# Gates by matmul, state tiles from chunk 2 on, a room of its own for the first x block, rows three deep, and a written plan of units

## The chip, the cores and the metric

One core of one Trainium2 chip runs the whole kernel in one launch. The metric is device time in microseconds (us): the median over runs of the same program. TensorE (PE) does matmuls into PSUM, VectorE (DVE) and ScalarE (ACT) work element by element, GpSimd (POOL) here mostly issues accumulating DMAs ("gathers"), and SyncE (SP) issues the other DMAs.

## What is computed

Sequence length S = 2048, width D = 1024, state width P = 1024, all in bf16. Two branches work on the same x and a gate g mixes them:

```python
g = sigmoid((x * gate_w).sum(-1, keepdims=True))
# branch A: a diagonal complex state space model
h = Lam_bar * h + x_t @ B_bar.T            # for t in range(2048)
a = 2 * (hseq @ Cmat.T).real + x * Dskip
# branch B: short convolution of k (4 taps), times v, then a long convolution by FFT
kv = short_conv(B_k) * B_v
y = irfft(rfft(kv, 2S) * rfft(ssm_k, 2S))[:S] + kv * ssm_D
b = x * y
out = g * a + (1 - g) * b
```

## The kernel before

The kernel has two phases.

The **chunk loop** does branch B's long convolution, eight chunks of 128 channels (loop at L906, the last chunk from L1003). In pass c it transforms chunk c+1 (`fwd_K`, `fwd_V`: matmuls psk and psv), multiplies the spectra of chunk c on VectorE (`products`: tiles G, wkh, BT, t), and transforms chunk c-1 back (`inverse`: matmuls psz), whose result goes through `cv` to the DRAM scratch `cv_scr`. The taps of chunk c+2 and its times-v stand between these. Between them stand tiles of branch A's input product: `Bu(i)` (L687) gives two half units ("tiles"), each 32 matmuls of 256 columns ("odd" and "even") and 4 or 8 small ones with `lamd`, evicted by ScalarE to U. Pass c >= 3 takes both tiles of `Bu(c - 3)`, the last chunk four tiles (`Bu(4)`, `Bu(5)`).

The **scan phase** (from L1029) does the rest of branch A. `order` (L672) lists 16 units (time block tb of 512 steps, state group g of 256 states); units 6 to 15 are left for this phase. `scan(tb, g)` (L720) is VectorE's recurrence over one unit: rotate (A, trn), four scan instructions (W), rotate back (hb), and the odd steps into U. Scan j is unit (j // 4, j % 4). `turn_C` (L1039) turns one of eight C tiles; ScalarE writes m, VectorE does the rest; two are run after each of scans 0 to 3. `Cy(tb, tl)` is an output row t_ = 4 tb + tl: 128 time steps, 32 matmuls psy of 512 columns, over the four scans of its block and all C tiles, evicted by `scale_a` with the gate as scale to ga.

Each row also needs branch B. `loads` (L784) brings the row of `cv_scr` to pbb and of x to xr; `scale_b` (L794) scales pbb by 1 - g and Dskip by g to gd (one buffer), and a gather adds gd to pbb; `finish` (L825) multiplies xr by pbb on VectorE, adds that to ga by another gather and stores ga. The gate of rows 0 to 7 is formed by `gate_products` (VectorE: gd = x row times gate_w) and `gate_sum` (ScalarE: a sum along the row, then two sigmoids); that of blocks 2 and 3 by `gate` (L654): 32 one-column matmuls with the transposed x block and `gwb`, then two sigmoids.

The order of each engine is fixed: `put` (L91) chains every instruction of an engine behind the one before it, in the order in which the program text emits them. So what the generators and the loop at L1128 emit first goes first, and an instruction that waits holds up everything behind it on its engine. `between` (L1088) puts up to two finishes and one gate product into a scan; `prepare` puts the gate sum and `scale_b` behind a scan; `on_pe` (L1123) lists TensorE's units, taken at 1.3 per scan.

Rooms: `xt_pool` (L78) has three buffers in turn for the angle table h, the two-chunk loads v2, the x blocks and U2. When the chunk loop's pools close (L1028), the pools of the scan phase are laid over them in the order m, lam2, uu2, hb, io, wk.

Of the kernel before, what the change touches and what calls it, by code (L numbers as in the profile page):

```python
# [20 lines left out]
def kernel(  # L21
# [38 lines left out]
    TB = 512  # L60
# [16 lines left out]
    bt_pool = pool("bt", 1)  # L77
    xt_pool = pool("xt", 3)  # L78
    uu = pool("uu", 2), pool("uv", 4)
# [133 lines left out]

    def load_xT(tb, home=None, halves=(0, 1)):
        if 0 in halves:
            xTs[tb] = (home or xt_pool).tile([128, ND, TB], BF16, name="xT", tag="xT")
        for h in halves:
            load_t(xTs[tb][:, :, h * HB:(h + 1) * HB], xf[tb * TB + h:(tb + 1) * TB:2, :])
# [98 lines left out]
    def inverse_angles():  # L317

        hi = inv["room"] = xt_pool.tile([128, 2, 512], F32, name="h", tag="xT")
        for fi in range(2):  # L320
            act(hi[:, fi], trow[0], func=ACT.Identity, scale=inv["col"][:, fi:fi + 1], bias=inv["at0"][:, fi:fi + 1])
        yield
        rq = u4([128, 1024], F32, "rq")
        ts(rq, flat(hi), MAGIC, -MAGIC, ALU.add, ALU.add)
        yield
        tt(flat(hi), flat(hi), rq, ALU.subtract)
# [305 lines left out]
    omg = consts.tile([128, NT], F32, name="omg")  # L632
    gsum = consts.tile([128, NT], F32, name="gsum")
    gds = {}
    hbs = {}
# [5 lines left out]
    def gates_of(c4, sums):  # L641
        act(gcols[:, c4], sums, func=ACT.Sigmoid)
        act(omg[:, c4], sums, func=ACT.Sigmoid, scale=-1.0)

    def gate_products(t_):
        xw = gds[t_] = s5p["io"].tile([128, D], BF16, name="gd", bufs=1)
        tt(xw, ios[t_][1], rows_, ALU.mult)

    def gate_sum(t_):
        xw = gds.pop(t_)  # L650
        act(xw, xw, func=ACT.Copy, accum_out=gsum[:, t_:t_ + 1])
        gates_of(slice(t_, t_ + 1), gsum[:, t_:t_ + 1])

# [33 lines left out]
    def Bu(i):  # L687
        tb, g = order[i]
        if i in (10, 11):
            if i == 10:  # L690
                s5p["u2"] = xt_pool.tile([128, 2, 2, 2, 2, HB], BF16, name="U2", tag="xT")
            U = s5p["u2"][:, i - 10]
        else:
            home = uu[0 if i in (0, 1, 12, 13) else 1] if i < 6 or i in (12, 13) else s5p["uu"]
            U = home.tile([128, 2, 2, 2, HB], BF16, name="U")
        Us[tb, g] = U
        return [Bu_tile(tb, g, U, j) for j in range(2)]
# [96 lines left out]
    def scale_b(t_):  # L794
# [5 lines left out]
        else:  # L800
            gd = bt_row(3, t_ - NT + 4)
        act(gd, s5p["drow"], func=ACT.Identity, scale=gcols[:, t_:t_ + 1])
        gather(pbb, gd)
# [15 lines left out]
    def scale_a(t_, ps):  # L819
# [3 lines left out]
        gas[t_] = ga  # L823

    def finish(t_, ps=None):  # L825

        rows = rows_of(of, t_)
        pbb, xr = ios.pop(t_)
        tt(xr, xr, pbb, ALU.mult)
        if t_ < NT - 4:  # L830
            ga = gas.pop(t_)
            gather(ga, xr)
            yield
        elif ps is None:
            yield
# [15 lines left out]
    def step(gen):  # L851
        next(gen, None)
# [50 lines left out]

    old = none

    for c in range(NC - 1):  # L906
# [41 lines left out]
        run(old)  # L948
        if c == 1:
            load_BT(1, 0)  # L950
        elif c == 3:
            load("v", 6)
            load_BT(1, 1)
        elif c in (2, 4, 6):
            load_xT(c // 2 - 1)
        if nn < NC:
            dg = dgs(nn)
        bu = Bu(c - 3) if c >= 3 else (none, none)
        step(bu[0])
        fwd_K(n, (0, 1))  # L960
        step(bu[0])
        fwd_K(n, (2, 3))
# [9 lines left out]
        if nn < NC:  # L972
            tv = times_v(nn)
            step(tv)
            if nn + 1 < NC:
                load("kn", nn + 1)
                load("kT", nn + 1)
        step(bu[1])
        fwd_V(n, (0, 1))
        step(bu[1])  # L980
        fwd_V(n, (2, 3))
        if c < 3:
            lam_diag(c - 1, lam_pool)
# [19 lines left out]
    with tc.tile_pool(name="fin", bufs=1, side="right") as fin:  # L1003
# [9 lines left out]
        run(back)  # L1013
        b0, b1 = Bu(4)
        step(b0)
        step(b1)
        step(b0)
        run(prod)
        b2, b3 = Bu(5)
        step(b2)  # L1020
# [6 lines left out]
        run(back)  # L1027
    h3.close()  # L1028
    m_pool = pool("m", 3)  # L1029
    lam_pool2 = pool("lam2", 1)  # L1030
    s5p["uu"] = pool("uu2", 4)
    s5p["hb"] = pool("hb", 7)
    s5p["io"] = pool("io", 2)
    wk = pool("wk", 6)

# [11 lines left out]

    move(rows_, bc(gate_w.rearrange("(o d) -> o d", o=1), [128, D]))
    loads(0)
    s5p["drow"] = s5p["io"].tile([128, D], BF16, name="drow", bufs=1)  # L1050
    move(s5p["drow"], bc(A_Dskip.rearrange("(o d) -> o d", o=1), [128, D]))
    load_CT(range(4, NP), "ctb")
    for g in (2, 3):
        lam_diag(g, lam_pool2, g == 3)
# [28 lines left out]
    NS = NTB * NG  # L1083
    done = []

    rows = dict(loaded=1, prepared=0)

    def between():  # L1088
        t_ = rows["next"] = rows["prepared"] if rows["prepared"] < rows["loaded"] else None
        if t_ is not None and t_ < 2 * NG:  # L1090
            gate_products(t_)
        for t_ in [t_ for t_ in done if t_ < rows["prepared"]][:2]:
            done.remove(t_)
            yield from finish(t_)
            if rows["loaded"] < NT - 4:
                loads(rows["loaded"])
                rows["loaded"] += 1

    def prepare():
        t_ = rows["next"]  # L1100
        if t_ is not None:
            if t_ < 2 * NG:
                gate_sum(t_)
            scale_b(t_)
            rows["prepared"] += 1

    scans = [scan(j // NG, j % NG, between() if j > 0 else none) for j in range(NS)]

# [6 lines left out]
    def Cy_row(k):  # L1115
        Cy(k // NG, k % NG)
        done.append(k)

# [3 lines left out]
    Bu_next(7)  # L1122
    on_pe = ([(Bu_next, i) for i in range(8, 12)] + [(Cy_row, k) for k in range(4)]  # L1123
             + [(Bu_next, 12), (Bu_next, 13), (Cy_row, 4), (Bu_next, 14), (Cy_row, 5), (Bu_next, 15)]
             + [(Cy_row, k) for k in range(6, 12)])
    at = 0
    step(scans[0])
    for j in range(NS):  # L1128
        k = j - NG
        if 6 <= k < 10:  # L1130
            loads(k + 6)
        advance(j)
        for t in turning[2 * j:2 * j + 2]:
            run(t)
        on_act += [lambda t=t: step(t) for t in turning[2 * j + 3:2 * j + 5] for _ in range(2)]
        if j > 0:
            prepare()
        if j in (1, 2):
            loads(j)
            rows["loaded"] = j + 1  # L1140
        while at < len(on_pe) and at < (j + 1) * 1.3:
            f, i = on_pe[at]
            f(i)
            at += 1
        if 7 <= k < 11:
            scale_b(k + 5)
        if j == 0:
            load_xT(3)
        if k in (4, 5):
            gate(k - 2)  # L1150

# [7 lines left out]
    for g in range(NG - 1):  # L1159
        for tl in range(4):  # L1160
            Cy_g(tb, tl, pss[tl][0], g, False)
    while rows["prepared"] < NT - 4:
        rows["next"] = rows["prepared"]
        prepare()
    for t_ in done:
        run(finish(t_))
    fins = []
# [36 lines left out]
```

## Time and profile before

| | us |
|---|---|
| median of 3 runs (lowest, highest) | 440.94 (440.88, 442.83) |
| the profiled execution | 441.8 |
| its span | 439.9 |
| TensorE busy | 404.0 (92%) |
| VectorE busy | 389.8 (89%) |
| ScalarE busy | 259.0 (59%) |
| GpSimd busy | 50.4 (11%) |
| mean granted TensorE clock | 0.966 |

The page divides the span into 40 equal slices of 11 us; a digit is the busy share in tenths, 9 for 90% or more:

```profile
PE   7999796959999999989989998659999999999996
PEld 5556262626767667655858887324486765444442
DVE  8699999999979898999959926999789999999874
ACT  5797687876698777562348769611555651664201
POOL 3011120302012010100000001001110100231300
PEclk9999898989999999998989999879999999999998
```

The slices from about 253 to 297 us (the 24th to the 27th) hold the lowest VectorE digit of the page, TensorE's 8, 6 and 5, and a clock digit of 7; in nearly all other slices one of the two engines stands at 9 (8 in two or three). TensorE's matmuls overlap in their records, so a group's busy time can be a little more than the time it took; where matmuls follow each other without a gap, the distance from start to start is the cost of one.

### The profile page before, as it was taken

Reading aid. Unit: us, or ns where it says so; the run is one execution under the profiler, and the core shown is the slowest. Engines: PE = TensorE matmul, PEld = TensorE weight load, DVE = VectorE, ACT = ScalarE, POOL = GpSimd, SP = SyncE. Lnnn points to the kernel's source line nnn. Section 1 sums busy time; section 2 is a strip of 40 time slices with the busy share of each in tenths; the row PEclk is TensorE's granted clock in tenths of the full one; section 3 lists DMA queues with packets and bytes.
Section 4 is the critical chain, followed back from the end, with each engine's and each line's share of the span. In section 5 each row is a group of like instructions: output and inputs, shape, how many; then the busy total and the mean of one; then the engine's idle time right before and its main releaser. Section 6 shows DMA issues by size and latency. Waiting matters only on the chain.

```text
span 439.9 us, 7369 instructions
## 1 busy us (share of the span) xinstructions
PE 404.0 (92%) x2894; PEld 255.6 (58%) x2921; DVE 389.8 (89%) x643; ACT 259.0 (59%) x360; POOL 50.4 (11%) x71
## 2 busy tenths in 40 slices
PE   7999796959999999989989998659999999999996
PEld 5556262626767667655858887324486765444442
DVE  8699999999979898999959926999789999999874
ACT  5797687876698777562348769611555651664201
POOL 3011120302012010100000001001110100231300
PEclk9999898989999999998989999879999999999998
DMA  8889799896969981669939951114661535795802
GB/s 145 145 181 207 189 202 125 167 192 138 215 129 136 168 183 24 132 87 178 182 129 169 172 130 25 25 24 114 152 127 48 115 94 145 167 218 134 175 26 96
DMA packets 126149, 59.49 MB, mean 135 GB/s; under 512 B 106009, under 2 KB 112929, under 8 KB 126114
## 3 DMA queue, kind: packets, MB, share of 16 engines
q1 hardware_dynamic: 117808, 42.48, 47.1%
q0 software_dynamic: 8224, 16.52, 22.4%
q8 instruction: 23, 0.38, 0.4%
q14 instruction: 12, 0.10, 0.1%
q10 hardware_dynamic: 82, 0.02, 0.0%
HBM read 13.13 MB, written 8.39 MB: 49 GB/s over the span
## 4 chain that ended last, share of the span: by engine, by line
PE 56%; DVE 25%; issue 10%; DMA 4%; ACT 3%; SPq 1%; DVEq 0%; POOLq 0%
PE psy L93 24%; PE psk L93 7%; PE even L93 7%; DVE BT L93 5%; PE psz L93 5%; PE odd L93 5%; DVE G L93 5%; DVE wkh L93 5%; PE taps L93 4%; DVE t L93 3%; PE psv L93 3%; DMA kn<-in_B_ssm_k_dram 1%; DVE CT L93 1%; DVE W L93 1%; ACT Vh L93 1%
## 5 line engine op out<-in xcount | busy, mean ns | idle before, releaser
L93 PEld LDWEIGHTS <-BT 128*128 128x128 bf16 x1024 | 99.9, 98 | 15.5 <-issue 2.3
L93 PE MATMUL psy<-CT,hb 128*128 128x512 bf16 x249 | 60.9, 397 | 8.5 <-DVE CT L93 4.5
L93 PE MATMUL even<-xT,BT 128*128 128x256 bf16 x512 | 61.1, 273 | 2.0 <-ACT U L93 2.0
L93 PE MATMUL odd<-xT,BT 128*128 128x256 bf16 x512 | 61.1, 273 | 0.0
L93 PE MATMUL psy<-CT,U 128*128 128x512 bf16 x251 | 56.3, 379 | 0.3
L93 PEld LDWEIGHTS <-hb 128*128 128x128 bf16 x256 | 25.9, 101 | 40.4 <-issue 14.1
L93 PEld LDWEIGHTS <-U 128*128 128x128 bf16 x256 | 25.0, 98 | 29.8
L93 PE MATMUL psz<-G,CI 128*128 128x512 bf16 x64 | 28.4, 444 | 15.0 <-DVE G L93 14.9
L93 ACT ACTIVATE Vh<-psv 128x1024 bf16<-128x1024 f32 x32 | 30.9, 1038 | 7.9 <-PE psv L93 7.9
L93 DVE TENSOR_TENSOR_SCAN W<-rv,init,A 128x256 bf16<-128x256 f32 x48 | 32.1, 729 | 0.0
L93 ACT ACTIVATE U<-even 128x512 bf16<-128x512 f32 x32 | 19.0, 593 | 21.4 <-PE even L93 21.3
L93 PE MATMUL taps<-dg,kT 128*128 128x128 bf16 x512 | 31.6, 224 | 0.0
L93 PEld LDWEIGHTS <-SF 128*128 128x128 bf16 x192 | 18.8, 98 | 20.8 <-issue 1.9
L93 PEld LDWEIGHTS <-kT 128*128 128x128 bf16 x512 | 30.2, 101 | 0.9
L93 ACT ACTIVATE U<-odd 128x512 bf16<-128x512 f32 x32 | 18.9, 594 | 18.7 <-PE odd L93 18.2
L93 PE MATMUL psk<-eok,SF 128*128 128x512 bf16 (+1 forms) x128 | 29.4, 353 | 0.4
L93 ACT ACTIVATE cv<-psz 128x1024 bf16<-128x1024 f32 x16 | 16.5, 1030 | 22.5 <-PE psz L93 22.5
L93 PE MATMUL psz<-G,SI 128*128 128x512 bf16 x64 | 28.7, 449 | 0.0
L93 ACT ACTIVATE ga<-psy,gcols 128x1024 bf16<-128x1024 f32 x8 | 8.9, 1112 | 33.2 <-PE psy L93 33.2
L93 POOL DMA_DIRECT2D pbb<-gd x12 | 10.7, 888 | 134.5 <-PE odd L93 83.1
L93 DVE TENSOR_TENSOR U<-U,q 128x512 bf16<-128x512 bf16 (+2 forms) x51 | 23.5, 488 | 0.6
L93 ACT ACTIVATE BT<-psy,gcols 128x1024 bf16<-128x1024 f32 x5 | 5.5, 1109 | 29.9 <-PE psy L93 29.9
(169 smaller groups left out, 770.9 us busy)
## 6 DMA issues: line engine op xcount, KB each, us to landing
G<-wkh POOLq DMA_DIRECT2D x6, 768.0 KB, 8.1
cv_scr<-cv SPq DMA_DIRECT2D x16, 256.0 KB, 2.7
v<-in_B_v_dram SPq DMA_DIRECT2D x3, 1024.0 KB, 14.7
pbb<-cv_scr SPq DMA_DIRECT2D x12, 256.0 KB, 3.9
xr<-in_A_x_dram SPq DMA_DIRECT2D x12, 256.0 KB, 3.7
pbb<-gd POOLq DMA_DIRECT2D x12, 256.0 KB, 4.1
ga<-xr POOLq DMA_DIRECT2D x8, 256.0 KB, 3.3
out_dram<-ga SPq DMA_DIRECT2D x8, 256.0 KB, 2.8
```

The source lines that it names most:

```text
L93: i = f(*a, **kw)
```

## The change

- `gate_products` and `gate_sum` are gone with their tiles; all four blocks get their gate by `gate`: blocks 0 to 2 in the last chunk, behind the first state tile there, block 3 in the scan phase at j = 8. `rows_` now holds Dskip in place of gate_w.
- State tiles are drawn one by one from a single list: one in pass 2, one in pass 3, two in pass 4, one in pass 5, three in pass 6, four in the last chunk (0, 2, 2, 2, 2, 4 before).
- `xt_pool` is split into one buffer (`xt_first`: h, x block 0, x block 3) and two in turn (v2, x blocks 1 and 2, U2). x block 0 is loaded in pass 1, v 6 and the first half of BT 1 in pass 2.
- The pools of the scan phase are laid out in the order wk, lam2, hb, m, uu2 (five buffers in place of four), io.
- `between` is now one `product` (xr times pbb) per scan from scan 3 on; `Cy_row(k)` emits the row, then its sum and store (`combine`), then the loads of row k + 3 and the scaling of row k + 2. Rows 0 to 2 are loaded ahead.
- `plan` says which B units and rows stand behind each scan. Unit 12 comes ahead of row 0.

```diff
--- before.py
+++ after.py
@@ -75,7 +75,7 @@
     rot_pool = pool("rot", 1)
     lam_pool = pool("lam", 1)
     bt_pool = pool("bt", 1)
-    xt_pool = pool("xt", 3)
+    xt_first, xt_pool = pool("xta", 1), pool("xtb", 2)
     uu = pool("uu", 2), pool("uv", 4)
     psum = pool("psum", 4, space=bass.MemoryType.PSUM)
 
@@ -211,9 +211,9 @@
     def load_BT(g, c):
         load_t(BT[g][:, c], (A_B_re, A_B_im)[c][g * 256:(g + 1) * 256, :])
 
-    def load_xT(tb, home=None, halves=(0, 1)):
+    def load_xT(tb, halves=(0, 1)):
         if 0 in halves:
-            xTs[tb] = (home or xt_pool).tile([128, ND, TB], BF16, name="xT", tag="xT")
+            xTs[tb] = (xt_pool if tb in (1, 2) else xt_first).tile([128, ND, TB], BF16, name="xT", tag="xT")
         for h in halves:
             load_t(xTs[tb][:, :, h * HB:(h + 1) * HB], xf[tb * TB + h:(tb + 1) * TB:2, :])
 
@@ -316,7 +316,7 @@
 
     def inverse_angles():
 
-        hi = inv["room"] = xt_pool.tile([128, 2, 512], F32, name="h", tag="xT")
+        hi = inv["room"] = xt_first.tile([128, 2, 512], F32, name="h", tag="xT")
         for fi in range(2):
             act(hi[:, fi], trow[0], func=ACT.Identity, scale=inv["col"][:, fi:fi + 1], bias=inv["at0"][:, fi:fi + 1])
         yield
@@ -630,8 +630,6 @@
 
     gcols = consts.tile([128, NT], F32, name="gcols")
     omg = consts.tile([128, NT], F32, name="omg")
-    gsum = consts.tile([128, NT], F32, name="gsum")
-    gds = {}
     hbs = {}
     WL, init = {}, {}
     for tb in range(NTB):
@@ -641,15 +639,6 @@
     def gates_of(c4, sums):
         act(gcols[:, c4], sums, func=ACT.Sigmoid)
         act(omg[:, c4], sums, func=ACT.Sigmoid, scale=-1.0)
-
-    def gate_products(t_):
-        xw = gds[t_] = s5p["io"].tile([128, D], BF16, name="gd", bufs=1)
-        tt(xw, ios[t_][1], rows_, ALU.mult)
-
-    def gate_sum(t_):
-        xw = gds.pop(t_)
-        act(xw, xw, func=ACT.Copy, accum_out=gsum[:, t_:t_ + 1])
-        gates_of(slice(t_, t_ + 1), gsum[:, t_:t_ + 1])
 
     def gate(tb):
         psg = ps2([128, 2, 512], "p")[:, 0, 0:4]
@@ -691,7 +680,7 @@
                 s5p["u2"] = xt_pool.tile([128, 2, 2, 2, 2, HB], BF16, name="U2", tag="xT")
             U = s5p["u2"][:, i - 10]
         else:
-            home = uu[0 if i in (0, 1, 12, 13) else 1] if i < 6 or i in (12, 13) else s5p["uu"]
+            home = uu[0 if i in (0, 1, 13, 14) else 1] if i < 6 or i in (13, 14) else s5p["uu"]
             U = home.tile([128, 2, 2, 2, HB], BF16, name="U")
         Us[tb, g] = U
         return [Bu_tile(tb, g, U, j) for j in range(2)]
@@ -799,7 +788,7 @@
             gd = s5p["io"].tile([128, D], BF16, name="gd", bufs=1)
         else:
             gd = bt_row(3, t_ - NT + 4)
-        act(gd, s5p["drow"], func=ACT.Identity, scale=gcols[:, t_:t_ + 1])
+        act(gd, rows_, func=ACT.Identity, scale=gcols[:, t_:t_ + 1])
         gather(pbb, gd)
 
     def Cy_g(tb, tl, ps, g, last):
@@ -822,16 +811,21 @@
             act(ga[:, o], i, func=ACT.Identity, scale=gcols[:, t_:t_ + 1])
         gas[t_] = ga
 
+    def product(t_):
+        pbb, xr = ios[t_]
+        tt(xr, xr, pbb, ALU.mult)
+
+    def combine(t_):
+        ga = gas.pop(t_)
+        gather(ga, ios.pop(t_)[1])
+        move(rows_of(of, t_), ga)
+
     def finish(t_, ps=None):
 
         rows = rows_of(of, t_)
-        pbb, xr = ios.pop(t_)
-        tt(xr, xr, pbb, ALU.mult)
-        if t_ < NT - 4:
-            ga = gas.pop(t_)
-            gather(ga, xr)
-            yield
-        elif ps is None:
+        product(t_)
+        xr = ios.pop(t_)[1]
+        if ps is None:
             yield
             ga = gas.pop(t_)
             tt(ga, ga, xr, ALU.add)
@@ -902,6 +896,7 @@
     fwd_V(0, (2, 3))
 
     old = none
+    tiles = (b for i in range(6) for b in Bu(i))
 
     for c in range(NC - 1):
         n, nn = c + 1, c + 2
@@ -947,18 +942,20 @@
         run(back)
         run(old)
         if c == 1:
+            load_xT(0)
+        elif c == 2:
+            load("v", 6)
             load_BT(1, 0)
         elif c == 3:
-            load("v", 6)
             load_BT(1, 1)
-        elif c in (2, 4, 6):
+        elif c in (4, 6):
             load_xT(c // 2 - 1)
         if nn < NC:
             dg = dgs(nn)
-        bu = Bu(c - 3) if c >= 3 else (none, none)
-        step(bu[0])
+        bu = next(tiles) if c >= 3 else none
+        step(bu)
         fwd_K(n, (0, 1))
-        step(bu[0])
+        step(bu)
         fwd_K(n, (2, 3))
         step(prod)
         fk = none
@@ -975,10 +972,13 @@
             if nn + 1 < NC:
                 load("kn", nn + 1)
                 load("kT", nn + 1)
-        step(bu[1])
+        bu = [next(tiles) for _ in range({2: 1, 4: 1, 6: 2}.get(c, 0))] + [none, none]
+        step(bu[0])
         fwd_V(n, (0, 1))
+        step(bu[0])
         step(bu[1])
         fwd_V(n, (2, 3))
+        step(bu[1])
         if c < 3:
             lam_diag(c - 1, lam_pool)
         old = tabs
@@ -1011,12 +1011,13 @@
         run(old)
         steps(prod, 3)
         run(back)
-        b0, b1 = Bu(4)
+        b0, b1, b2, b3 = tiles
         step(b0)
+        for tb in range(3):
+            gate(tb)
         step(b1)
         step(b0)
         run(prod)
-        b2, b3 = Bu(5)
         step(b2)
         step(b1)
         step(b3)
@@ -1026,12 +1027,12 @@
         step(b3)
         run(back)
     h3.close()
+    wk = pool("wk", 6)
+    lam_pool2 = pool("lam2", 1)
+    s5p["hb"] = pool("hb", 7)
     m_pool = pool("m", 3)
-    lam_pool2 = pool("lam2", 1)
-    s5p["uu"] = pool("uu2", 4)
-    s5p["hb"] = pool("hb", 7)
+    s5p["uu"] = pool("uu2", 5)
     s5p["io"] = pool("io", 2)
-    wk = pool("wk", 6)
 
     def w2(shape, dt, name):
         return wk.tile(shape, dt, name=name, tag="w2")
@@ -1045,11 +1046,10 @@
             ts(CT[pi][:, c], CT[pi][:, c], f[:, pi:pi + 1], None, ALU.mult)
         tt(CT[pi], CT[pi], m, ALU.add)
 
-    move(rows_, bc(gate_w.rearrange("(o d) -> o d", o=1), [128, D]))
     loads(0)
-    s5p["drow"] = s5p["io"].tile([128, D], BF16, name="drow", bufs=1)
-    move(s5p["drow"], bc(A_Dskip.rearrange("(o d) -> o d", o=1), [128, D]))
+    move(rows_, bc(A_Dskip.rearrange("(o d) -> o d", o=1), [128, D]))
     load_CT(range(4, NP), "ctb")
+    loads(1)
     for g in (2, 3):
         lam_diag(g, lam_pool2, g == 3)
     late = []
@@ -1081,30 +1081,19 @@
 
 
     NS = NTB * NG
-    done = []
-
-    rows = dict(loaded=1, prepared=0)
+    rows = dict(scaled=0, multiplied=0)
 
     def between():
-        t_ = rows["next"] = rows["prepared"] if rows["prepared"] < rows["loaded"] else None
-        if t_ is not None and t_ < 2 * NG:
-            gate_products(t_)
-        for t_ in [t_ for t_ in done if t_ < rows["prepared"]][:2]:
-            done.remove(t_)
-            yield from finish(t_)
-            if rows["loaded"] < NT - 4:
-                loads(rows["loaded"])
-                rows["loaded"] += 1
+        if rows["multiplied"] < rows["scaled"]:
+            product(rows["multiplied"])
+            rows["multiplied"] += 1
+        yield
 
     def prepare():
-        t_ = rows["next"]
-        if t_ is not None:
-            if t_ < 2 * NG:
-                gate_sum(t_)
-            scale_b(t_)
-            rows["prepared"] += 1
-
-    scans = [scan(j // NG, j % NG, between() if j > 0 else none) for j in range(NS)]
+        scale_b(rows["scaled"])
+        rows["scaled"] += 1
+
+    scans = [scan(j // NG, j % NG, between() if j > 2 else none) for j in range(NS)]
 
     def advance(j):
         step(scans[j])
@@ -1114,40 +1103,36 @@
 
     def Cy_row(k):
         Cy(k // NG, k % NG)
-        done.append(k)
+        combine(k)
+        if k + 3 < NT - 4:
+            loads(k + 3)
+        if k + 2 < NT - 4:
+            prepare()
 
     turning = [turn_C(pi) for pi in range(NP)]
     on_act += [lambda t=t: step(t) for t in turning[0:3] for _ in range(2)]
     Bu_next(6)
     Bu_next(7)
-    on_pe = ([(Bu_next, i) for i in range(8, 12)] + [(Cy_row, k) for k in range(4)]
-             + [(Bu_next, 12), (Bu_next, 13), (Cy_row, 4), (Bu_next, 14), (Cy_row, 5), (Bu_next, 15)]
-             + [(Cy_row, k) for k in range(6, 12)])
-    at = 0
+    plan = ["B8", "B9 B10", "B11", "B12 C0", "C1", "C2", "C3", "B13", "C4 B14", "C5", "B15 C6", "C7", "C8", "C9", "C10", "C11"]
     step(scans[0])
     for j in range(NS):
-        k = j - NG
-        if 6 <= k < 10:
-            loads(k + 6)
+        if 10 <= j < 14:
+            loads(j + 2)
         advance(j)
         for t in turning[2 * j:2 * j + 2]:
             run(t)
         on_act += [lambda t=t: step(t) for t in turning[2 * j + 3:2 * j + 5] for _ in range(2)]
-        if j > 0:
+        for unit in plan[j].split():
+            (Bu_next if unit[0] == "B" else Cy_row)(int(unit[1:]))
+        if 0 < j < 3:
             prepare()
-        if j in (1, 2):
-            loads(j)
-            rows["loaded"] = j + 1
-        while at < len(on_pe) and at < (j + 1) * 1.3:
-            f, i = on_pe[at]
-            f(i)
-            at += 1
-        if 7 <= k < 11:
-            scale_b(k + 5)
+        if 11 <= j < 15:
+            scale_b(j + 1)
         if j == 0:
             load_xT(3)
-        if k in (4, 5):
-            gate(k - 2)
+            loads(2)
+        if j == 8:
+            gate(3)
 
     tb = NTB - 1
     t0 = tb * 4
@@ -1159,11 +1144,6 @@
     for g in range(NG - 1):
         for tl in range(4):
             Cy_g(tb, tl, pss[tl][0], g, False)
-    while rows["prepared"] < NT - 4:
-        rows["next"] = rows["prepared"]
-        prepare()
-    for t_ in done:
-        run(finish(t_))
     fins = []
     for tl in range(4):
         fins.append(finish(t0 + tl, None if tl == 1 else pss[tl][1]))
```

## The prediction

> **What bounds the kernel now.** I read three views: busy time by stage (stage borders at the inverse transforms of the chunks, at the end of the last product, 221.6 us, and at the first unbroken run of output rows, 294.6 us), then TensorE's and VectorE's instructions in order of time, then the chain of waits. Columns of the first: window, its length, busy us of PE, PE weight load, DVE, ACT, POOL with instruction counts, granted clock, DMA share, GB/s.
>
> ```profile
> 71.70:96.20 24.50, 19.41 (x131) 10.57 (x133) 24.43 (x27) 18.97 (x28) 3.95 (x5) 0.93 0.92 167
> 96.20:123.40 27.20, 27.09 (x203) 17.69 (x206) 25.48 (x27) 17.06 (x25) 3.95 (x5) 0.94 0.98 177
> 123.40:148.90 25.50, 25.39 (x204) 17.29 (x205) 23.51 (x20) 21.02 (x32) 3.95 (x5) 1.00 1.00 136
> 174.70:198.80 24.10, 21.49 (x146) 13.60 (x147) 22.63 (x20) 14.51 (x18) 1.20 (x1) 1.00 0.59 100
> 198.80:221.60 22.80, 20.86 (x168) 15.93 (x168) 22.70 (x19) 6.64 (x11) 0.00 (x0) 0.93 1.05 191
> 221.60:294.60 73.00, 62.76 (x515) 48.87 (x517) 54.95 (x116) 47.34 (x74) 2.61 (x3) 0.93 0.50 96
> 294.60:365.90 71.30, 70.15 (x536) 46.51 (x540) 64.47 (x145) 32.60 (x54) 9.50 (x11) 0.98 0.44 101
> 365.90:435.70 69.80, 69.42 (x324) 31.71 (x328) 61.10 (x138) 25.59 (x25) 12.06 (x14) 1.00 0.60 143
> ```
>
> In the chunk loop VectorE fills chunk 2 (24.43 of 24.50 us) and chunk 7, TensorE fills chunks 3 and 4. From 294.6 us TensorE is full to the end. The one stage that nobody fills is 221.6 to 294.6: 10 us of TensorE idle and 18 of VectorE. TensorE's idle there:
>
> ```profile
> 221.72 0.39 PE L93 MATMUL psz<-G,CI 128*128 128x512 bf16 x1 [2.06 <-DVE G L93]
> ...
> 274.78 1.91 PE L93 MATMUL even<-xT,BT 128*128 128x256 bf16 x16 [1.71 <-ACT U L93]
> ...
> 280.68 0.59 PE L93 MATMUL psy<-CT,hb 128*128 128x512 bf16 x1 [3.45 <-ACT U L93]
> ...
> 292.58 1.87 PE L93 MATMUL psy<-CT,hb 128*128 128x512 bf16 x4 [4.34 <-DVE CT L93]
> ```
>
> Output rows (psy) come too early: row 0 needs scans 0 to 3 and all eight turned C tiles, and VectorE is late with them. Why it is late, in its own order:
>
> ```profile
> 227.56 0.69 DVE L93 TENSOR_TENSOR A<-TCS,U 128x1024 bf16<-128x1024 bf16 x1 [4.92 <-PE psz L93]
> ...
> 267.91 0.69 DVE L93 TENSOR_TENSOR gd<-xr,rows 128x1024 bf16<-128x1024 bf16 x1 [12.40 <-ACT U L93]
> ...
> 320.86 0.69 DVE L93 TENSOR_TENSOR gd<-xr,rows 128x1024 bf16<-128x1024 bf16 x1 [4.76 <-issue]
> ```
>
> Scan 0 waits 4.92 us for the last inverse, whose tables lie in the room of its work tile; scan 2 waits 12.40 us for the single gd buffer. The chain shows that buffer's release:
>
> ```profile
> 264.62 3.21 DMA pbb<-gd
> 267.91 0.69 DVE gd L93
> ```
>
> The releaser printed (ACT U) had ended; the gather pbb<-gd ended last.
>
> **The change, part by part.** Let T0 be the end of the last product, 221.6 in this trace; the span ends 218.3 us later.
>
> *Gates.* Out go, for 8 rows, a VectorE product (0.60 us start to start), a ScalarE sum (1.05 + 0.19) and two sigmoids (0.2 each). In come gates of blocks 0 and 1 on TensorE, 32 one-column matmuls each: the two in the trace (blocks 2, 3) take 0.78 us from first to last start (349.51 to 350.29). Three stand in chunk 7: 2.35 us. TensorE's work there grows from 20.9 to 23.2, beside 22.9 of VectorE; the inverse that ends the stage waits 2.06 us in before, so this is hidden to within 0.3, and costs 2.35 if that wait is gone. The table load (1.28) moves there too, on a ScalarE busy 6.6 of 22.8 us. Gate 2 leaves the full stretch: -0.8.
>
> *State tiles from chunk 2 on.* A tile is 32 matmuls at 109 ns and 4 (block 0) or 8 small ones: 3.93 to 4.03 us. Per chunk 0,2,2,2,2,4 (chunks 2 to 7) become 1,1,2,1,3,4. Each chunk ends when both TensorE's transforms and VectorE's product are done, so I go chunk by chunk. Chunk 2: TensorE 19.4 + 3.9 = 23.3 beside 24.4, free (the 1.02 us that it waits there for ks<-lo is covered by the tile). Chunk 3: product 98.2 to 120.5, so the next inverse starts at 120.6 rather than 123.4: -2.8. Chunk 4, TensorE-bound, keeps 25.5. Chunk 5: TensorE 25.7 - 4.0 = 21.7, VectorE 22.4 from a start 1.3 us after the previous transform: another -2. Chunk 6 gives back: TensorE 21.6 + 4.0 = 25.6 beside 22.6. Carried through: last product starts at 196.2 instead of 198.6 (-2.4). But TensorE idles about 2 us before chunks 4 and 6, and rows of this trace halve the clock for 3.41 us after idles of 2.06 us and more (after 1.71 not): 1.7 each on a TensorE-bound chunk, so +0.9 at the other end. Bounds -2.5 to +0.9; I take -1.0.
>
> The Trainium skill, "TensorE: Matmul & The Clock Gate", Part 1, says that the half rate follows at least one idle window of about 3.4 us. By that the 2 us idles would cost nothing and this term would be -2.4; the trace has a halving after 2.06 us, so the row decides.
>
> *Transfers.* x block 0 (two transposes; SyncE's queue was held 11.3 us by them) moves ahead of kn 4 and kT 4 into chunk 1, in place of one B transpose (6.9): +4.4 to 5.6 us on those behind it. kT 4 left the queue at 72.2, lands about 4.6 later, and is used at 84.1: 7 us of cover. v 6 (1 MB, 14.7 to landing) moves from chunk 3 to 2, ahead of kn 5 and kT 5, whose cover is 10 us. Cost 0; without the cover up to 6. DMA share is 0.92 to 1.00 there, hence a rival.
>
> *Room order.* Scan 0's work tiles move off the tables: its instruction loses its wait on TensorE. VectorE starts 4.9 us earlier.
>
> *Rows.* xr*pbb now comes from scan 3 on, one per scan, and the finished scale of row k+2 is issued behind row k. The new wait: xr*pbb stands in VectorE's order, and behind it the rest of its scan. For row 0 ScalarE gets to it after tile pair B10, at T0+44.6 (inverse 4.15, then B6, B7 at 7.86, B8, B9 at 8.06, one and a half tiles more, an eviction); 2.2 to scale, 3.6 from there to VectorE as for row 0 above: T0+50.4. VectorE, free of gd, reaches it at T0+41.0: 0.85 for the lamd tile, 13.7 for scan 0 (227.56 to 241.26 here), twice 12.95 (241.26 to 254.82 less the gd product), 0.6. So it still waits, 9.4 us.
>
> *Plan of units.* B12 goes ahead of row 0: TensorE has 4.15 + 15.7 + 32.2 + 8.1 = 60.2 us of work before rows. VectorE after that wait ends scan 3 and the last two turns (2.05 each) 12.8 later, T0+63.2. Row 0 wants C tile 7 after 24 matmuls at 216 ns, T0+65.4. So the idles of the stage go: 0.25 + 1.71 + 3.45 + 0.22 + 4.34 + 0.19 + 0.91 = -11.1. With them go the half-rate clocks that follow the two long ones (280.5 to 283.9 and 290.8 to 297.6): 10.24 us at half, -5.1.
>
> Next late: scans take 9.8 us (10.15 with a carry), rows 6.9, B pairs 8.06. Rows 4 and 5 start at 95.9 and 111.6; scan 7's state is there at 99.9, wanted at 101.6: fits. xr*pbb of rows 7 and 8 waits for rows 5 and 6 plus 7.3 (1.1 eviction, 2.2 scales, 4.0 gather): 2.6 and 5.8 us. So scan 11's state comes at T0+148, and row 8 wants it at T0+145.6: +2.4 idle. Bounds 0 (a landing of 3.2, other waits absorbed) to 6 (landing 5.1 three times in a row). The last scan ends at T0+190, its state wanted at T0+192: TensorE sets the end.
>
> Sum on this execution: 439.9 - 1.0 - 11.1 - 5.1 - 0.8 + 2.4 = 424.3 us of span. 1.9 us lie around the span (441.8), and the median of the three runs is 0.9 below that run: **425 us**.
>
> **Rivals.**
> *All cover holds*: no idle at row 8, conversion of chunk gains in full, no halving before the last inverse (1.7): 424.3 - 2.4 - 1.4 - 1.7 = 418.8, 420 as a run. For: 2 us margins in the sums. Against: three margins under 2.5 us have all to hold. 0.12.
> *The round trip sets VectorE*: row, eviction, scale, gather, product, scan. With landings of 8.6 us (eok<-lo in the chunk loop) in place of 3.6 to 4.1, row 0 waits 2.8 for C tile 7, row 4 about 3, row 8 about 7: 13 in place of 2.4, and the clock is halved after them (3.4): 439 as a run at the worst, 436 with one absorbed. For: new waits on VectorE's path. Against: DMA share is 0.44 to 0.60 in these stages. 0.12.
> *A late kT or x block in chunks 2 to 5*: +4 to 6, 430. x block 1 landed about 0.4 us before its use in chunk 5. 0.08.
> *Slower*: gathers on POOL starve while VectorE runs. Then each of 12 products stops VectorE for a whole issue and landing, 0.86 + 3.3 = 4.2 us: 50 us less 4 of slack, 471. It passes before's time from (440.9 - 425.3 + 4) / 12 = 1.6 us per product. For: products were off this path before. Against: POOL's issue takes 0.86 us with VectorE full and 0.90 with it idle:
>
> ```profile
> 264.62 0.90 POOL L93 DMA_DIRECT2D pbb<-gd  x1 [83.14 <-PE odd L93]
> ```
> ```profile
> 374.97 0.86 POOL L93 DMA_DIRECT2D ga<-xr  x1 [9.99 <-ACT ga L93]
> ```
>
> 0.07. (The Trainium skill, "SBUF — State Buffer", section "SBUF: two separate sides", states such a rule: a VectorE mode that takes both ports locks GpSimd out, and its DMAs wait for their descriptors. The two rows don't show it.)
>
> **How the numbers follow.** Forecast 0.61 (421 to 429), and as above. 0.5% (2.2 us) is about what a measurement tells from no change: faster 0.90, same 0.03 (the round trip just past its worst), slower 0.07. The range 418 to 437 takes in the first rival and the round trip and leaves out the slow one.
>
> **What would show it.** Right: the idles at 274 to 294 are gone; VectorE stands about 9 us before the first xr*pbb; one idle of 1 to 4 us in row 8; TensorE full from T0+5; chunk 3 ends near 120.6; T0 within 219 to 222.5. Wrong: an idle before row 0 (VectorE's sum was short), a wait on kT or xT in chunks 2 to 5, landings over 5 us in the rows, or clock halvings with no idle of 2 us before them.

## The result and the profile after

The kernel after takes 428.69 us (median of 4 runs, 424.40 to 431.18); the kernel before, beside it, 441.88. The ratio is 0.967, 95% interval 0.958 to 0.975; it is taken of the fast runs alone, which leaves out the slow run of 431.18. A second set of six runs later gave 430.88 (427.89 to 432.71) beside 440.94: 0.978, 0.973 to 0.982. So it is faster by 2 to 4%, and its runs spread by 7 us.

The profiled run is one of the fastest: 424.40 us, with a span of 422.6 us against the 424.3 of span that the forecast's sum gave. Its stages, cut at its own borders; first in the chunk loop (chunks 3, 4 and 6), then from the end of the last product, 221.1 us, on. Columns as in the prediction: window, its length, busy us of PE, PE weight load, DVE, ACT, POOL with counts, granted clock, DMA share, GB/s.

```profile
95.30:119.70 24.40, 21.62 (x167) 13.63 (x169) 24.33 (x27) 21.34 (x33) 3.95 (x5) 1.00 1.18 194
119.70:147.30 27.60, 25.61 (x204) 17.23 (x207) 23.48 (x21) 20.13 (x30) 3.95 (x5) 1.00 1.02 126
...
170.80:198.20 27.40, 25.46 (x183) 17.24 (x186) 23.55 (x21) 14.62 (x19) 1.20 (x1) 1.00 0.80 87
...
221.10:294.60 73.50, 73.33 (x629) 58.39 (x632) 64.20 (x139) 45.60 (x66) 3.47 (x4) 1.00 0.53 99
294.60:365.90 71.30, 71.03 (x483) 43.47 (x487) 62.93 (x139) 29.63 (x35) 11.13 (x13) 1.00 0.60 137
```

The stage that nobody filled is full now: 73.33 of 73.50 us of TensorE where before had 62.76 of 73.00, and the clock in it is 1.00 instead of 0.93. Chunk 3 has become short (24.4 us, 27.2 before), but chunks 4 and 6 have become long (27.6 and 27.4, 25.5 and 24.1 before); chunk 6 also has one tile more than before. TensorE in order of time, last column the idle before the instruction and its releaser:

```profile
280.65 2.54 PE L93 MATMUL psy<-CT,hb 128*128 128x512 bf16 x10
```
```profile
368.04 2.33 PE L93 MATMUL psy<-CT,hb 128*128 128x512 bf16 x9 [1.28 <-DVE hb L93]
```

Row 0 starts with no idle before it, and of all idles behind the last product one is left, 1.28 us in row 8. VectorE, the two places that matter:

```profile
140.72 1.23 DVE L93 TENSOR_TENSOR G<-G,wkh 128x2048 bf16<-128x2048 bf16 x1 [4.09 <-DMA G<-wkh]
```
```profile
271.03 0.69 DVE L93 TENSOR_TENSOR xr<-xr,pbb 128x1024 bf16<-128x1024 bf16 x1 [7.46 <-DMA pbb<-gd]
```

The first is new: in chunk 4 the product waits for its own gather. The second is the wait for the first row's gather, which the prediction put at 9.4 us.

A reading that all the rest uses: call T0 the end of the last product on VectorE. The span is T0 plus the stage behind it. Busy time by stage (same columns) of the kernel after:

```profile
0.00:221.10 221.10, 200.10 (x1617) 128.94 (x1633) 207.70 (x246) 155.69 (x214) 26.24 (x43) 0.98 0.95 156
221.10:422.60 201.50, 195.22 (x1340) 124.66 (x1352) 177.97 (x391) 93.40 (x118) 24.02 (x28) 1.00 0.57 123
```

Before: T0 221.66, VectorE busy 207.91 of it, and 218.24 us behind it. So nearly the whole gain (16.7 us of 17.3 in the profiled runs) comes from behind T0, and up to T0 VectorE works for 207.7 us and waits for the other 13.4. T0 moves with waits.

### The profile page after: what moved, and what is told of

The parts are those of the page before. It is cut to its first block, busy times and chain, and to the rows that moved or that the text cites. A ratio compares the mean times of both kernels' runs of the same rounds, so it can differ in the third digit from the quotient of the medians.

```text
span 422.6 us, 7462 instructions
## 1 busy us (share of the span) xinstructions
PE 395.3 (94%) x2957; PEld 253.6 (60%) x2985; DVE 385.7 (91%) x635; ACT 249.1 (59%) x332; POOL 50.3 (12%) x71
## 4 chain that ended last, share of the span: by engine, by line
DVE 35%; issue 34%; PE 16%; DMA 11%; POOL 2%; ACT 2%; DVEq 0%; POOLq 0%; SPq 0%
DMA G<-wkh 8%; DVE BT L93 7%; PE psy L93 6%; DVE wkh L93 6%; DVE G L93 6%; DVE t L93 4%; PE psk L93 3%; DVE W L93 2%; DMA pbb<-cv_scr 2%; PE psz L93 2%; DVE hb L93 1%; DVE A L93 1%; PE taps L93 1%; DVE q L93 1%; DVE trn L93 1%
## 5 line engine op out<-in xcount | busy, mean ns | idle before, releaser
L93 PEld LDWEIGHTS <-BT 128*128 128x128 bf16 x1024 | 100.0, 98 | 13.4
L93 PE MATMUL psy<-CT,hb 128*128 128x512 bf16 x249 | 56.8, 379 | 1.6 <-DVE hb L93 1.3
L93 PEld LDWEIGHTS <-hb 128*128 128x128 bf16 x256 | 24.8, 98 | 30.4 <-DVE hb L93 2.0
L93 PE MATMUL psz<-G,CI 128*128 128x512 bf16 x64 | 26.1, 408 | 16.2 <-DVE G L93 16.2
L93 PE MATMUL psz<-G,SI 128*128 128x512 bf16 x64 | 25.9, 404 | 0.0
L93 PEld LDWEIGHTS <-CI 128*128 128x128 bf16 x64 | 6.6, 103 | 26.6 <-DVE G L93 19.1
```

The costliest lines, as they stand in the source:

```text
L93: i = f(*a, **kw)
```

## The experiments

Each is cut by its T0 and the time behind it, read from its trace, as well as by its run time.

**State tiles as before**, within the kernel after:

```diff
-        bu = [next(tiles) for _ in range({2: 1, 4: 1, 6: 2}.get(c, 0))] + [none, none]
+        bu = [next(tiles) for _ in range({3: 1, 4: 1, 5: 1, 6: 1}.get(c, 0))] + [none, none]
```

> The changed kernel with the state tiles handed out as before (0, 2, 2, 2, 2, 4 in chunks 2 to 7). Theory: the new places give almost nothing, because in the changed kernel VectorE waits 4.09 and 3.75 us in chunks 4 and 6 for the gather G<-wkh that lands late; the end of the last product (221.0 us in the changed kernel's trace) moves by 0 to +2 us, the time by as much. Rival (the prediction's chunk sums without any loss): chunk 3 and 5 become TensorE-bound again, +2.5 to +5 us.

427.85 us (4 runs, 422.42 to 432.79), T0 225.73, behind it 201.5. No difference from 428.69 that the spread lets one see. In its trace T0 is 4.6 us later than in after, which is the rival's range and not the theory's, but the runs as a whole are no longer; and a transfer was late there (TensorE waits 4.12 us for kT). The places of the tiles are worth nothing that can be measured here.

**Rooms of the scan phase as before** (m, lam2, uu2, hb, io, wk):

```diff
-    wk = pool("wk", 6)
-    lam_pool2 = pool("lam2", 1)
...
+    s5p["io"] = pool("io", 2)
+    wk = pool("wk", 6)
```

> The changed kernel with the pools of the scan phase laid out in the old order, so scan 0 waits again some 4.9 us for the last inverse. Theory: the wait of 7.46 us before the first xr*pbb takes this up whole (it shrinks to about 2.6), time 0 +- 0.5 us. Rival: VectorE's early start is what gets row 0 its C tiles in time; row 0 then waits 2 to 3 us, with a halved clock after it +4 us.

431.62 us (426.54 to 434.4), T0 223.29, behind it 201.5: to 0.1 us the time of after. The order of the rooms changes nothing behind T0. Scan 0 waits for no inverse in this trace either, so the wait that the new order was to remove did not come back here, and what the expectation said of it was not put to the test. The pool uu2 keeps its fifth buffer in this run, so wk does not lie where it lay in the kernel before; whether that is why stays open.

**B12 behind row 3**, within the kernel after:

```diff
-    plan = ["B8", "B9 B10", "B11", "B12 C0", "C1", "C2", "C3", "B13", "C4 B14", "C5", "B15 C6", "C7", "C8", "C9", "C10", "C11"]
+    plan = ["B8", "B9 B10", "B11", "C0", "C1", "C2", "C3", "B12 B13", "C4 B14", "C5", "B15 C6", "C7", "C8", "C9", "C10", "C11"]
```

> The changed kernel with unit 12 behind row 3, where it stood before, and nothing else moved. Theory: row 0 reaches its last C tile 8 us earlier than VectorE has turned it, less a margin of 2.5: TensorE idles 5 to 6 us in row 0 and the clock is halved after it, +5 to +9 us. Rival: TensorE's work is the same and rows only trade places, 0 to +1 us.

435.77 us (435.01 to 438.02, 7 runs), behind T0 208.7, 7.2 more. TensorE in order of time:

```profile
287.79 1.86 PE L93 MATMUL psy<-CT,hb 128*128 128x512 bf16 x4 [3.61 <-DVE CT L93]
```

The idle on the C tiles in row 0 is back, 3.61 us, and a half-rate window of 3.41 us right behind it costs 1.7 more. Another 1.7 of the 7.2 is a half-rate window from 226.3 us on, behind an idle of 2.26 us before the last inverse, and has nothing to do with B12. In this row pipeline B12 ahead of row 0 is needed.

**Gates from TensorE alone**, in the kernel before: old tiles, rooms, rows and order of units.

```diff
         step(b0)
+        for tb in range(3):
+            gate(tb)
         step(b1)
...
-        if t_ is not None and t_ < 2 * NG:
-            gate_products(t_)
...
-            if t_ < 2 * NG:
-                gate_sum(t_)
...
-        if k in (4, 5):
-            gate(k - 2)
+        if k == 5:
+            gate(3)
```

> The kernel before with one part of the change: gates of blocks 0 to 2 by matmul in the last chunk, of block 3 in the scan phase, no gate product on VectorE and no sum on ScalarE (the broadcast load of gate_w stays, unused). Theory: the 12.40 us wait of VectorE was for the gd buffer of the gate product alone, so it goes, row 0 finds its C tiles within 0 to 3 us, and this part alone brings 10 to 15 us of the 17 between the two profiled spans: 427 to 432. Rival: the wait moves to xr*pbb, and the plan of units and the rows in a pipeline carry the gain; this part alone brings 4 to 8 us: 434 to 438.

425.06 us (423.49 to 428.94), ratio 0.965 (0.959 to 0.972): as fast as the whole change or faster, and below the range of either forecast. T0 225.35, behind it 201.8, and TensorE has no idle at all there, though B12 stands behind row 3 as before. VectorE's wait of 5.13 us for the last inverse, which is gone in after, is still there and leaves TensorE without an idle.

**A tile of its own for the gates' product**, in the kernel before, gates left where they were:

```diff
-        xw = gds[t_] = s5p["io"].tile([128, D], BF16, name="gd", bufs=1)
+        xw = gds[t_] = s5p["io"].tile([128, D], BF16, name="gp", bufs=1)
```

> The kernel before, with one edit: the gates' product x*gate_w gets a tile of its own, so that it no longer waits until the gather pbb<-gd has read the single gd buffer. The gates stay on VectorE and ScalarE. Theory A (the gates cost by that wait and the TensorE idles and half-rate clocks behind it, not by their work): the 12.40 us wait of VectorE before the second product shrinks to under 3 us, the stage from the end of the last product to the end of the kernel, 218.2 us in before and 201.8 with the gates on TensorE, comes to 202 to 207 us. Theory B (the work itself costs: eight sums and sigmoids on ScalarE ahead of the state evictions, eight products on VectorE): it stays at 212 us or more.

434.83 us (432.61 to 440.25), ratio 0.985 (0.979 to 0.990), T0 224.91, behind it 208.0: outside both forecasts, nearer to theory A. VectorE:

```profile
262.14 0.69 DVE L93 TENSOR_TENSOR gp<-xr,rows 128x1024 bf16<-128x1024 bf16 x1 [7.57 <-ACT gp L93]
```

The wait fell from 12.40 to 7.57 us, not under 3: the product no longer waits for the gather, but its single tile is still held by ScalarE's sum over the previous product, which stands in ScalarE's order between evictions. Behind T0 the tile of its own brings 10.2 of the 16.4 us that the gates cost there (218.2 to 208.0 to 201.8). Of the 10.2, 1.7 is chance: before has a half-rate window at 222.7 to 226.1 us behind an idle of 2.06 us, and here an idle of 2.04 us at the same place has none behind it (the last section has the reason). So sharing gd cost some 8.5 us.

**Products and sums kept, results unused** (gates from TensorE by the edits of the fourth experiment, old gd; this is the edit besides):

```diff
     def gate_sum(t_):
         xw = gds.pop(t_)
         act(xw, xw, func=ACT.Copy, accum_out=gsum[:, t_:t_ + 1])
-        gates_of(slice(t_, t_ + 1), gsum[:, t_:t_ + 1])
```

> The kernel before with the gates from TensorE, but with the old products on VectorE and sums on ScalarE still run, in the old gd buffer, their result unused (only their two sigmoids per row are left out). Theory A (the shared gd buffer): VectorE still waits over 8 us at the second product, and from the end of the last product to the end it takes 213 to 218 us. Rival C (what cost was that the row's scale waited for sums and sigmoids, the table load of 1.28 us with them): without the sigmoids on the path the wait ends earlier, 202 to 208 us.

One run, 436.80 us; behind T0 213.8, in theory A's range. VectorE:

```profile
264.22 0.69 DVE L93 TENSOR_TENSOR gd<-xr,rows 128x1024 bf16<-128x1024 bf16 x1 [10.65 <-ACT U L93]
```

Products and sums whose results nobody reads cost 12.0 of the 16.4 us, and the run before shows that most of that is the shared buffer. Of the other 4.4, 1.7 is again the half-rate window at 222.7 us, which is missing here; that the rest is the sigmoids and the table load is not shown.

**x blocks copied instead of transposed**, in the kernel after (blocks 0 to 2):

```diff
-            load_t(xTs[tb][:, :, h * HB:(h + 1) * HB], xf[tb * TB + h:(tb + 1) * TB:2, :])
+            move(xTs[tb][:, :, h * HB:(h + 1) * HB],
+                 xf[tb * TB + h * HB:tb * TB + (h + 1) * HB, :].rearrange("(p a) (m t) -> p (a m) t", a=2, t=HB))
```

> The kernel after, with the six transposing loads of x blocks 0 to 2 replaced by plain copies of as many bytes from the same rows (so the state inputs of these blocks are computed from wrongly ordered numbers; every instruction on the engines is the same). In the five traces so far VectorE is busy 207.7 to 208.0 us before the end of the last product, and that end, 221.1 to 225.7, differs by VectorE's waits alone, which go back to late gathers (ks<-lo, G<-wkh). Theory D (the transposes hold the DMA engines and delay the gathers): waits fall to under 9 us in all, the last product ends at 212 to 218 us, and the run takes 415 to 421 us. Rival E (the gathers are late on their own, or TensorE is what is late): 219 to 226 us as before, 422 to 431 us as a run.

428.46 us (421.88 to 429.36), T0 222.65. Theory D falls as it stands: no gather was late in chunks 4 and 6 in this trace, but T0 did not move; VectorE waited 2.43 and 4.28 us for Vh at the start of the products of chunks 5 and 7 instead. The times are rival E's, though its first reason, gathers late on their own, is not what the trace shows.

**xr*pbb behind the scan instructions**, in the kernel after:

```diff
+        yield
         if rows["multiplied"] < rows["scaled"]:
             product(rows["multiplied"])
             rows["multiplied"] += 1
-        yield
```

> The kernel after, with xr*pbb of a row put behind the scan instructions of its tile (four scans, 2.43 us, and two adds, 0.75 us) instead of ahead of them. Theory A: the idle of TensorE in row 8 (1.28 us in after, 1.26 in two other traces) comes from xr*pbb waiting for its gather with the scan behind it; 3.2 us later it waits under 1 us for rows 7 and 8, the idle goes, and from the end of the last product to the end it takes 200.0 to 200.6 us in place of 201.5. Rival F (the scans are late by their own sum): the idle stays within 0.3 us of 1.28 and the time at 201.2 to 201.8.

One run, 425.61 us; behind T0 200.21 us, theory A's 200.0 to 200.6. The idle in row 8 is gone, here and in the two later traces with this edit: it came from xr*pbb with the scan queued behind it, as the prediction had it.

The last four ran on one chip, side by side.

> The kernel after once more, beside the next three on one chip. If its time is the fixed stage behind the last product (201.5 us in four traces) plus a chunk loop that varies from run to run (last product at 221.1 to 225.7 us), its runs spread over 423 to 431 us with a median of 425 to 429, as before.

430.88 us (427.89 to 432.71, 6 runs), T0 224.47 in the profiled run, behind it 201.6. The stages are as forecast; the median is 1.9 us above the forecast's upper end and the slowest run 1.7.

> The kernel before with the gates from TensorE alone, once more. Theory A (the gates carry the whole gain; tiles, rooms, rows and plan bring nothing that can be measured): its median is within 2 us of after's in this call. Rival (the rest of the change was worth the 1.0 us in the chunk loop that the prediction gave it, or more, and was hidden by the spread): after's median is lower by over 2 us.

423.37 us (422.96 to 425.21, 6 runs), ratio to before 0.961 (0.958 to 0.964), where after has 0.978 (0.973 to 0.982) beside it. Both theories are wrong: the rest of the change is worth less than nothing, some 7.5 us in the median, and none of after's six runs is as fast as the slowest of the gates alone. The two profiles, the kernel after first, up to T0 and behind it:

```profile
0.00:224.47 224.47, 203.17 (x1631) 129.77 (x1632) 207.69 (x246) 154.85 (x213) 26.21 (x43) 0.98 0.98 153
224.47:426.10 201.63, 196.07 (x1357) 124.70 (x1355) 177.92 (x391) 94.04 (x119) 24.01 (x28) 1.00 0.56 123
```
```profile
0.00:221.33 221.33, 204.76 (x1630) 130.44 (x1631) 207.96 (x246) 154.75 (x213) 26.21 (x43) 0.97 0.89 157
221.33:421.50 200.17, 195.92 (x1359) 124.77 (x1355) 177.35 (x391) 93.40 (x119) 24.41 (x28) 1.00 0.54 123
```

Of 4.6 us between them 3.1 lie in T0 and 1.5 behind it (1.25 of these are row 8's idle). The 3.1 is not firm: the other trace of the gates alone has its T0 at 225.35. VectorE is busy equally long; what differs is its waits. DMA share up to T0 is 0.98 against 0.89 for nearly the same bytes. In chunk 4, the issue of the product's gather (POOL) and of x block 1's transposes (SP), and the gather's line in the table of DMA issues (KB, us from issue to landing), first of the kernel before, then of after's first profile:

```profile
129.15 1.20 POOL L93 DMA_DIRECT2D G<-wkh  x1 [12.98 <-DVE wkh L93]
```
```profile
131.26 7.53 SPq L93 DMA_TRANSPOSE xT<-in_A_x_dram  x1
```
```profile
G<-wkh POOLq DMA_DIRECT2D x1, 768.0 KB, 9.8
```
```profile
124.97 1.20 POOL L93 DMA_DIRECT2D G<-wkh  x1 [9.75 <-DVE wkh L93]
```
```profile
125.29 17.48 SPq L93 DMA_TRANSPOSE xT<-in_A_x_dram  x2
```
```profile
G<-wkh POOLq DMA_DIRECT2D x1, 768.0 KB, 15.7
```

The chunk has moved up by 4 us, as the tile taken from chunk 3 was to bring about. But the gather and the transposes now start 0.3 us apart instead of 2.1, and the gather takes 15.7 us instead of 9.8 (18.1 in after's second profile; 9.3 with the gates alone). In chunk 6 it takes 16.0 us against 11.7. The transposes close behind it are the cause: in the three traces in which they start 0.3 to 0.4 us behind the gather (after's two and the eighth experiment's) it takes 15.7 to 18.1 us in both chunks, wherever they start 2.1 us behind it 6.9 to 9.8, and with plain copies 0.3 us behind it 9.1. In these profiles the gain of chunk 3 is given back in chunk 4.

That does not make the late gather the cause of a late T0. Three other traces have after's chunk loop unchanged and no late gather in chunks 4 and 6 (old order of rooms, B12 behind row 3, and the next run): their T0 is 223.3, 225.2 and 224.6, where the three with late gathers have 221.1, 223.6 and 224.5. VectorE waits for Vh there instead (4.3 us before the product of chunk 7 in each).

> The kernel after with xr*pbb behind the scan instructions, timed. The stage behind the last product again takes 200.0 to 200.6 us; the median is 0 to 3 us under after's (1.3 expected, on a spread of 7).

428.23 us (425.40 to 429.61), 2.7 under after. Behind T0 201.7, outside the forecast: TensorE idled 2.26 us for the last product, and a half-rate window fell behind T0 (+1.7); without it 200.0. In this profile the gathers of chunks 4 and 6 are in time (9.0 and 6.9 us).

**No gather in chunks 4 and 6**, on top of the run before it:

```diff
-        tabs, back, prod = turn_table(c - 1) if c <= NG else none, inverse(c - 1), products(c)
+        tabs, back, prod = turn_table(c - 1) if c <= NG else none, inverse(c - 1), products(c, by_dma=c not in (4, 6))
```

> As the run before it, but in chunks 4 and 6 the product's first partial sum is added by VectorE (1.67 us more in each) instead of by a gather, for which VectorE waited 4.09 and 3.75 us in after and 4.98 and 4.82 with xr*pbb behind the scan. Theory G (that late gather is what the chunk loop waits for): those waits go, the last product ends at 216 to 219 us, and the median is 416 to 421 us. Rival H (VectorE and TensorE take turns in the chunk loop, and another wait, of G for Vh from ScalarE, takes its place, as in the traces with the old rooms or the old plan: 3.4 to 6.4 us at chunk 4 or 6): the last product ends at 221 to 226 us and the median is 422 to 429 us.

427.68 us (422.26 to 429.81), T0 220.38, between the two forecasts. The median is in rival H's range and moved by 0.6 us only. No gather is left to wait for in chunks 4 and 6, 3.4 us of adds have come in, and VectorE waits 0.76 and 2.60 us for Vh. As the run before it had no late gather in its profile, the step from 224.58 to 220.38 is not the gather's doing. Taking the gather away does not make the kernel as fast as with the gates alone.

## Why the prediction was right, and where it was not

The forecast, 425 us, is within 1% of 428.7, and the likeliest case (421 to 429) is the one that came, at its upper end; the second set, 430.88, lies above that case. The stage behind T0 was forecast by its mechanism; that the total of the profiled run fits so well (422.6 us of span, 424.3 forecast) owes something to an early T0 and to one half-rate window. By its steps:

- *The idles before row 0 and the half-rate windows behind them* (-11.1, -5.1): they are gone, as forecast, though the gates alone remove them (see the plan of units). Behind T0 the sum gave 218.2 - 11.1 - 5.1 - 0.8 + 2.4 = 203.6; the trace has 201.5. Row 0 starts at T0+59.6 (60.2 forecast); the first xr*pbb at T0+49.9 (50.4), after 7.46 us of waiting (9.4). Of the 2.1 us between, 1.1 is the next point, and 1.7 a half-rate window behind T0 in before (222.7 to 226.1), whose end the sum left out; smaller things go the other way.
- *Row 8* (+2.4): right in place and cause, as the eighth experiment shows; the size was 1.28.
- *Gates*: 96 one-column matmuls take 2.41 us (2.35 forecast) beside VectorE (the two times read for the forecast are ends of matmuls, not starts; their difference is the same). That the single gd buffer was the main cause is shown (some 8.5 us of 16.4), with an addition: behind the gather stood a second wait, for ScalarE's sum (7.57 us with a tile of its own).
- *Room order* ("VectorE starts 4.9 us earlier"): scan 0 does start without that wait, but in the run with the old order it does too, so the order is not shown to be the reason; and it is worth nothing. With the gates alone scan 0 still waits 3.46 us, and TensorE has no idle.
- *Plan of units*: in after, B12 ahead of row 0 is needed, as the third experiment shows. That it mends what the new rows cause is argued and not tried: they put xr*pbb into scan 3, where VectorE waits 7.46 us; with the old rows and the old order there is no such wait before 301 us. The prediction credited the plan and the room order with idles that the gates alone remove.
- *State tiles and transfers* (-1.0, "Transfers ... Cost 0"): this is the step that did not hold. Chunk 3 ended at 119.7 (120.6 forecast), but moving chunk 4 up set its gather right ahead of the transposes of x, and the gain went into a wait of 4.09 us (6.51 in the second profile). So the transfers were not free; the transfer rival (0.08) named kT and x blocks as what would be late, and in after's profiles it was the accumulating gather. T0 came 0.6 us earlier in one profile and 2.8 us later in the next (bounds were -2.5 to +0.9). The old chunk loop, with the gates added in its last chunk, varies as much from trace to trace (221.2, 221.3, 225.4), so the term of 1 us can be neither confirmed nor refuted by T0, and that it came out at -0.6 in the first profile is luck.
- *Signs of being wrong*: one came, half-rate windows without an idle of 2 us before them (46.6 us in the profiled run, behind 1.81; 211.1 in the second, behind the gates). And T0 of the second profile, 224.47, lies outside the 219 to 222.5 that would have shown the forecast right.
- *Slower, gathers starving on POOL*: didn't happen. In after nine of the twelve xr*pbb in the scans wait under 1 us. The page "SBUF — State Buffer" of the Trainium skill, section "SBUF: two separate sides", states the lock of which the prediction made this rival; these waits do not show it.

What stays open: why the whole change is 7.5 us slower in the median than the gates alone. Row 8's idle is 1.25 of it. The late gather is in after's profiles, but T0 is no earlier in traces without it. After's runs without a profile in the second set are longer than its profiled one (median of all six 430.9 beside 427.9), at a granted clock of 0.970 to 0.980 instead of 0.988. By an estimate from these clocks, at 1.7 us for each window, some two to five more half-rate windows would give that; where they fall no trace shows. Neither the new loads in chunks 1 and 2 nor the new rows were tried alone.

The gates alone, 423.37 us, are faster than both kernels.

## What to carry to other kernels

Cut a pipelined kernel at the point where its limit changes and compare stages, not totals: here one stage repeats to 0.2 us in four traces and the other varies by 5, and a sum that fits can hide a part that loses. A one-buffer tile shared by two steps ties their engines together; here the product in it takes 0.69 us, and the wait for it was 12.40. Pulling a stage forward also moves its transfers: look at which other transfer they will start beside.

## What the runs showed of the hardware

**TensorE's half rate goes by a fixed grid.** In all 14 traces every half-rate window begins on one grid of 3.413 us, whose place differs from run to run. Call a window of this grid a cell. Up to the last instructions there are 1655 full-rate cells with another cell behind them. All 61 with 2.04 us or more without a matmul were followed by a half-rate cell; of the 1594 with 2.00 us or less, 5 were (two with 1.81 and 1.84, where others with as much were not, and three with no idle at all). So the same idle counts or not by where it falls. PE busy, clock, DMA share and GB/s by grid cell; in the kernel before, around an idle of 2.06 us, and in after, around one of 2.70:

```profile
219.27:222.68 3.41, 1.35 (x10) 1.00 1.02 276
222.68:226.09 3.41, 3.41 (x16) 0.50 0.00 0
```
```profile
114.90:118.31 3.41, 2.12 (x10) 1.00 1.22 256
118.31:121.72 3.41, 1.99 (x10) 1.00 1.02 194
121.72:125.13 3.41, 3.41 (x24) 1.00 0.20 77
```

The first lies within one cell, and the next cell is at half rate; the second is split into 1.28 and 1.42, and no cell behind it is. The prediction's reading ("after idles of 2.06 us and more") was too simple. The page "TensorE: Matmul & The Clock Gate" of the Trainium skill, Part 1, says that the window is free-running, which these rows bear out. The idle window of about 3.4 us that it gives is longer than the 2.04 us seen here.

**A half-rate window can follow the gates without any idle.** The three exceptions without idle stand right behind the 96 one-column gate matmuls, during which TensorE is busy by the profile. Here is after's second profile, with the gates at 208.54 to 211.09, all in one cell, and then the eighth experiment's, with 2.22 us of them in the first cell:

```profile
207.71:211.12 3.41, 3.41 (x108) 1.00 1.15 194
211.12:214.53 3.41, 3.41 (x18) 0.50 1.58 153
```
```profile
208.16:211.57 3.41, 3.41 (x102) 1.00 1.19 210
211.57:214.98 3.41, 3.41 (x43) 1.00 1.32 100
```

Twelve traces have these 96 matmuls. In the three with 2.43 us or more of them in one cell the half rate followed, and in the nine with at most 2.23 it did not. So matmuls this thin seem to count as idle, with a border (between 2.23 and 2.43 us) a little above that of a true idle (about 2 us). That is read from three cases, and no run was made to test it. In the run of the gates alone where the window came, it stood before T0 (213.7 to 217.1), scan 0 waited 5.13 us for the last inverse and the stage behind T0 took 201.8 us; where it did not come, 3.46 and 200.2.
